# A new order for a fused attention and gated-MLP kernel: loads of q on SyncE's queue, work moved between engines

## The chip, the cores and the metric

One core of a Trainium2 chip runs the whole program. The metric is the time of one execution on the device in microseconds, the median of several runs. The engines are TensorE (PE, with its weight loads shown as PEld), VectorE (DVE), ScalarE (ACT), GpSimd (POOL) and SyncE (SP, which here only issues DMAs).

## The reference

The inputs are q, k and v of shape 4 x 8 x 768 x 64 (batch, heads, sequence, head size), a decay per head and the weights of a gated MLP. All come in float32, and so does the output of shape 4 x 768 x 512.

```python
# linear attention with decay, in blocks of 64 positions
intra = einsum('bhic,bhjc->bhij', qb, kb) * Dmask      # lam ** (i - j), causal
intra = einsum('bhij,bhjd->bhid', intra, vb)
inter = einsum('bhid,bhde->bhie', qb * lam_pow, kv_state)
out[:, :, sl] = intra + inter
kv_state = lam_block * kv_state + einsum('bhsd,bhse->bhde', kb_dec, vb)
# gated MLP with spatial mixing; x is the attention's output, 4 x 768 x 512
h = maximum(x @ w_in, 0);  u, v = halves of h
v_n = (v - mean(v)) / sqrt(var(v) + 1e-6)
v_s = einsum('ts,bsd->btd', w_spatial, v_n) + b_spatial
return (u * v_s) @ w_out
```

## The kernel before, in words

The work is cut into twelve steps of 256 positions, three for each of the four batches. Step n belongs to batch n // 3. All matmuls are in bf16.

Nothing is scheduled by a compiler: the string ORDER lists some 650 tokens, and the program issues them one after the other. A token such as `GM.0.3.0.D` is an operation (GM), its indices (batch 0, feature tile 3, half 0) and, in its last letter, the engine: T for TensorE, D for VectorE, A for ScalarE, P for GpSimd, S for a DMA that SyncE issues. Each engine works its own tokens strictly in this order; between engines, semaphores follow from which tile an instruction reads or writes. So a token that waits holds up all that stands behind it on its engine. Eight semaphores in turn tell of the landing of DMAs from SyncE and ScalarE, so one of these DMAs is issued only after the one eight before it has landed.

The operations that the text names, with their lines:

- LQ, LK, LV (`load`, L191): the float32 loads of q, k and v of one step, 512 KB each as given by the profile, into one of three buffers each.
- WI, WS, WO (L257, L262, L266): loads of the weights by GpSimd, cast to bf16. GT (`after`, L253) copies one number out of a loaded tile on GpSimd, so that the weights behind it are not asked for before that load has landed.
- WU (`w_u`, L212): filler matmuls of 256 columns on a constant tile, whose result nobody reads.
- KC, QC, QM (L178 or L176, L299): q and k to bf16 in another layout; QM also scales q. TK, TQ (L328) transpose on TensorE, EK, EQ bring the result to SBUF (EQ with the decay). From step 7 on, the DMAs DK and DQ (L305, L309) transpose instead.
- VD (L314): v scaled by the decay, in two halves; both inputs are in SBUF.
- SC (L369): the scores, two halves of a step; MK (L373): score times mask, PSUM to SBUF.
- KV (L385): the state, accumulated in PSUM bank 7; SS (L176): its copy to SBUF (`s_sb`). The next KV waits for SS, since it writes the same bank.
- AV.n.0 and AV.n.1 (L406, L415): the attention output. Between them stands SY (`apart`), a copy of two numbers on DVE or ACT, for which AV.n.1 waits. EX copies the result to SBUF as `xT`.
- PV (L438), EV, BN, RA, RD (L466 is its second instruction, with two SBUF inputs, 128x2 elements), VN: the second half of h and its normalization.
- PU (L485), EU (L443): the first half of h, transposed.
- WT, EW: the transposed spatial weights. PW (L506): the spatial matmul. GB (L511): its result plus bias, PSUM to SBUF (`vsb`, two buffers). GM (L517): `vsb` times `uT`; both inputs are in SBUF.
- PO (L522), PH (L528): the last matmul; EO, EH: its copy into one of six output tiles (`o_sb`); ST, SH: the store. An output tile is written again for the next batch, after its store.

Of the kernel before, what the change touches and what calls it, by code (L numbers as in the profile page):

```python
# [25 lines left out]
EU.0.1.3.A AV.2.0.0.T RD.0.D PU.1.0.5.T SS.2.0.A SY.2.0.D BN.1.1.D AV.2.1.0.T PU.0.0.2.T EX.2.0.0.A EX.2.1.1.D
RA.1.A VN.0.0.D VN.0.1.A PV.2.1.1.T BS.S RD.1.0.D VN.1.0.D EU.0.0.2.A PV.2.0.0.T QC.3.2.D EV.2.1.1.A VN.1.1.D
PU.2.0.6.T EV.2.0.0.A BN.2.1.D EU.1.0.5.A LK.4.2.S TQ.3.1.T BN.2.0.D EU.2.0.6.A WT.1.3.T WT.2.0.T KC.3.2.P
EQ.3.1.D RA.2.A WT.5.4.T EW.2.0.A WT.4.2.T RD.2.0.D LV.4.2.S WT.0.6.T EW.4.2.D EW.5.4.A WT.3.1.T TK.3.0.T
EW.1.3.D QC.4.2.P EW.0.6.D PU.2.1.2.T EK.3.0.A LQ.5.2.S EW.3.1.D TQ.4.6.T VN.2.1.D EU.2.1.2.A VN.2.0.D  # L30
SC.3.0.0.T VD.3.0.D SC.3.1.3.T PW.0.1.1.5.T LK.5.2.S MK.3.1.3.D PW.0.0.0.2.T GB.0.1.1.5.D LK.6.2.S GM.0.1.1.P
PW.0.0.1.4.T GB.0.0.0.2.D MK.3.0.0.D KC.4.2.P PW.0.1.0.3.T LV.5.2.S EQ.4.6.D GM.0.0.0.P PW.0.3.1.2.T
GB.0.0.1.4.D VD.3.1.P TK.4.5.T GB.0.1.0.3.D PW.0.2.0.4.T GB.0.3.1.2.D LQ.6.2.S EK.4.5.A GM.0.1.0.P KV.3.0.T
AV.3.0.0.T GM.0.0.1.P SC.4.1.2.T SS.3.0.A SC.4.0.5.T SY.3.0.D GB.0.2.0.4.D LV.6.2.S KV.3.1.T AV.3.1.0.T
QC.5.2.P MK.4.1.2.D PW.0.3.0.4.T EX.3.0.0.A EX.3.1.1.A GM.0.3.1.P MK.4.0.5.D TQ.5.0.T LQ.7.2.S KC.5.2.A
PU.3.1.1.T VD.4.1.P EQ.5.0.D SS.3.1.A TK.5.2.T VD.4.0.P GB.0.3.0.4.D PU.3.0.6.T EK.5.2.A EU.3.1.1.D KV.4.0.T
LV.7.2.S VD.5.1.P EU.3.0.6.A AV.4.0.0.T SS.4.0.D SC.5.0.4.T SY.4.0.D LK.7.2.S WO.P SC.5.1.2.T VD.5.0.P
KV.4.1.T MK.5.0.4.D AV.4.1.0.T PV.3.1.6.T LK.8.2.S EX.4.0.0.A QC.6.2.P MK.5.1.2.D EX.4.1.1.A PV.3.0.5.T
KC.6.2.A GM.0.3.0.D PV.4.1.0.T LQ.9.2.S EV.3.1.6.A TQ.6.3.T BN.3.1.D EV.4.1.0.A QM.7.1.P TK.6.1.T PU.4.1.2.T
BN.4.1.D VD.6.1.P PU.4.0.4.T EQ.6.3.D EU.4.1.2.A QM.7.0.P SS.4.1.D EV.3.0.5.A PW.0.2.1.6.T EK.6.1.D EU.4.0.4.A  # L40
VD.6.0.P KV.5.0.T GB.0.2.1.6.D AV.5.0.0.T SS.5.0.A SC.6.0.4.T GM.0.2.0.P SC.6.1.2.T SY.5.0.A KV.6.0.T
AV.5.1.0.T MK.6.1.2.D PV.4.0.6.T EX.5.1.1.A DQ.7.S EX.5.0.0.A BN.3.0.D PO.0.2.1.T KC.7.2.P MK.6.0.4.D RA.3.A
PV.5.1.0.T EV.4.0.6.A VD.7.0.P DK.7.S SS.6.0.A PV.5.0.2.T BN.4.0.D EO.0.2.1.A GM.0.2.1.P PO.0.1.4.T RD.3.D
LQ.8.2.S EV.5.0.2.A VD.7.1.P RA.4.A PO.0.0.3.T VN.3.0.D EV.5.1.0.A EO.0.1.4.A AV.6.0.5.T BN.5.0.D KV.6.1.T
ST.0.1.S PU.5.0.4.T SS.6.1.A LV.8.2.S EO.0.0.3.A SY.6.5.D RD.4.D QM.9.1.P KV.7.0.T BN.5.1.D EU.5.0.4.A
AV.6.1.5.T PO.0.5.3.T ST.0.0.S VN.4.1.D EX.6.0.5.A SS.7.0.D RA.5.A EX.6.1.6.A PU.5.1.0.T RD.5.D VN.4.0.A
SC.7.1.1.T LV.9.2.S EU.5.1.0.D VN.3.1.A SC.7.0.5.T KV.7.1.T PO.0.3.4.T MK.7.0.5.D QM.8.0.P VN.5.1.A PV.6.0.0.T
SS.7.1.D EO.0.3.4.A QM.8.1.P MK.7.1.1.D KC.8.2.A PO.0.4.5.T DQ.8.S EO.0.5.3.A PV.6.1.6.T VD.8.0.P VD.8.1.D
VN.5.0.A PU.6.1.4.T LK.9.2.S EO.0.4.5.A DK.8.S QM.9.0.P AV.7.0.1.T EV.6.1.6.A KV.8.0.T EU.6.1.4.A SY.7.1.D
BN.6.1.D AV.7.1.1.T EV.6.0.0.A PW.1.0.1.6.T DQ.9.S VD.9.1.P EX.7.1.2.A BN.6.0.D SS.8.0.A PW.1.1.0.0.T VD.9.0.P  # L50
EX.7.0.1.D LQ.10.2.S PW.1.1.1.5.T GB.1.1.0.0.D ST.0.4.S GB.1.0.1.6.D PV.7.1.3.T GB.1.1.1.5.D KC.9.2.A
GM.1.0.1.P PW.1.0.0.2.T EV.7.1.3.A GM.1.1.1.P DK.9.S RA.6.A KV.9.0.T BN.7.1.D SC.8.0.5.T GM.1.1.0.P SC.8.1.0.T
PV.7.0.3.T GB.1.0.0.2.D ST.0.2.S MK.8.1.0.D PU.7.0.4.T EV.7.0.3.A RD.6.D PU.7.1.2.T EU.7.0.4.D LK.10.2.S
BN.7.0.D PW.1.3.1.0.T ST.0.3.S QM.10.0.P RA.7.A PU.6.0.1.T VN.6.1.A RD.7.D GM.1.0.0.P GB.1.3.1.0.D
PW.1.2.1.3.T EU.6.0.1.A MK.8.0.5.D LK.11.2.S EU.7.1.2.A PW.1.2.0.4.T LQ.11.2.S SS.9.0.A GB.1.2.1.3.D ST.0.5.S
AV.8.0.0.T GM.1.2.1.P GB.1.2.0.4.D SC.9.1.2.T KV.9.1.T SY.8.0.A SC.9.0.5.T VN.7.0.A MK.9.1.2.D AV.8.1.0.T
GM.1.3.1.P PW.1.3.0.4.T EX.8.1.1.A QM.10.1.P MK.9.0.5.D EX.8.0.0.A PO.1.3.2.T VN.6.0.A DQ.10.S GB.1.3.0.4.D
PV.8.1.1.T VN.7.1.D GM.1.3.0.P GM.1.2.0.D PV.8.0.3.T LV.10.2.S EV.8.1.1.A PU.8.1.6.T EV.8.0.3.A EO.1.3.2.A
PO.1.0.4.T BN.8.0.D PO.1.1.5.T QM.11.1.P BN.8.1.D EO.1.0.4.A EU.8.1.6.A PO.1.2.0.T ST.1.0.S KC.10.2.P ST.1.3.S
RA.8.A EO.1.1.5.A RD.8.D PO.1.5.2.T ST.1.1.S VN.8.0.D VN.8.1.A PU.8.0.4.T DK.10.S EO.1.2.0.A PW.2.0.1.3.T  # L60
SS.9.1.A VD.10.0.P EU.8.0.4.A LV.11.2.S PW.2.1.1.0.T ST.1.2.S VD.10.1.P GB.2.0.1.3.D GM.2.0.1.D PO.1.4.5.T
# [523 lines left out]
```

## Time and profile before

| | us |
|---|---|
| median of 3 runs | 156.41 |
| the runs | 155.68 to 156.83 |
| the profiled execution | 155.68 |
| its span, from first to last instruction | 154.0 |
| PE busy in it | 137.1 |
| of that, 61 fillers (L212) | 9.2 |
| DVE busy | 106.1 |
| ACT busy | 89.9 |
| POOL busy | 69.8 |

The lines of the profile below start with a line of the kernel and an engine, or with a time. In a timeline, the first number is the start in us from the span's start, the second the duration. In a table of stretches, a row gives the stretch, its length, then for PE, PEld, DVE, ACT and POOL the busy time and the number of instructions, then the granted clock of TensorE, the DMA share and GB/s. The mean granted clock of TensorE was 0.989.

### The profile page before, as it was taken

Reading aid. Unit: us, or ns where it says so; the run is one execution under the profiler, and the core shown is the slowest. Engines: PE = TensorE matmul, PEld = TensorE weight load, DVE = VectorE, ACT = ScalarE, POOL = GpSimd, SP = SyncE. Lnnn points to the kernel's source line nnn. Section 1 sums busy time; section 2 is a strip of 40 time slices with the busy share of each in tenths; the row PEclk is TensorE's granted clock in tenths of the full one; section 3 lists DMA queues with packets and bytes.
Section 4 is the critical chain, followed back from the end, with each engine's and each line's share of the span. In section 5 each row is a group of like instructions: output and inputs, shape, how many; then the busy total and the mean of one; then the engine's idle time right before and its main releaser. Section 6 shows DMA issues by size and latency. Waiting matters only on the chain.

```text
span 154.0 us, 4860 instructions
## 1 busy us (share of the span) xinstructions
PE 137.1 (89%) x2060; PEld 90.5 (59%) x2075; DVE 106.1 (69%) x191; ACT 89.9 (58%) x167; POOL 69.8 (45%) x83
## 2 busy tenths in 40 slices
PE   6967774969999999839999999999999999999990
PEld 4746542456876786635565657655676756565540
DVE  1247724688999679989976778885469888748300
ACT  3968373566850677417799824678373647960270
POOL 7435650055008999827255564564644002014700
PEclk9999998799999999999999999999999999999999
DMA  3999999999999969965999997999797000052364
GB/s 91 300 290 289 237 241 235 220 281 257 281 285 285 257 169 280 235 165 105 231 282 172 245 233 184 320 201 288 164 292 172 2 6 0 0 198 79 136 231 178
DMA packets 54152, 31.25 MB, mean 203 GB/s; under 512 B 11634, under 2 KB 51058, under 8 KB 54130
## 3 DMA queue, kind: packets, MB, share of 16 engines
q1 hardware_dynamic: 49520, 27.01, 68.6%
q0 software_dynamic: 2384, 2.75, 10.3%
q10 hardware_dynamic: 2226, 1.18, 3.0%
q8 instruction: 16, 0.26, 0.7%
q14 instruction: 6, 0.05, 0.1%
HBM read 24.77 MB, written 6.29 MB: 202 GB/s over the span
## 4 chain that ended last, share of the span: by engine, by line
PE 68%; DVE 10%; DMA 9%; SPq 6%; ACT 2%; issue 2%; POOL 1%; DVEq 0%
PE ps L506 19%; PE ps L522 13%; PE ps L438 11%; PE ps L485 10%; DMA q_in<-in_q_dram 9%; SPq L191 6%; DVE gT L517 3%; PE ps L369 3%; PE ps L415 3%; DVE a_sb L373 2%; PE ps L328 2%; PE ps L385 2%; PE ps L406 2%; PE ps L498 1%; POOL vd L314 1%
## 5 line engine op out<-in xcount | busy, mean ns | idle before, releaser
L517 POOL TENSOR_TENSOR gT<-vsb,uT 128x384 bf16<-128x384 f32 x24 | 21.8, 917 | 40.1 <-DVE vsb L511 31.4
L506 PE MATMUL ps<-wt_sb,vn 128*128 128x384 bf16 x192 | 33.9, 326 | 0.0
L373 DVE TENSOR_TENSOR a_sb<-ps,m 128x1024 bf16<-128x1024 f32 x24 | 28.6, 1216 | 2.2 <-PE ps L369 1.9
L314 POOL TENSOR_TENSOR vd<-v_in,lv 128x512 bf16<-128x512 f32 x19 | 19.6, 1043 | 18.5 <-DVE a_sb L373 10.7
L506 PEld LDWEIGHTS <-vn 128*128 128x128 bf16 x192 | 18.3, 98 | 11.9
L485 PE MATMUL ps<-xT,win_sb 128*128 128x256 bf16 x192 | 24.4, 273 | 0.0
L438 PE MATMUL ps<-win_sb,xT 128*128 128x512 bf16 x87 | 23.6, 400 | 0.4
L511 DVE TENSOR_TENSOR vsb<-ps,bsp 128x384 f32<-128x384 f32 x32 | 17.2, 550 | 9.5 <-PE ps L506 9.5
L522 PE MATMUL ps<-wout_sb,gT 128*128 128x512 bf16 x86 | 21.4, 379 | 0.4 <-issue 0.2
L443 ACT ACTIVATE vh<-ps 128x512 bf16<-128x512 f32 x23 | 13.7, 596 | 13.4 <-PE ps L438 12.4
L485 PEld LDWEIGHTS <-win_sb 128*128 128x128 bf16 x192 | 18.4, 98 | 4.9
L174 ACT ACTIVATE o_sb<-ps 128x512 f32<-128x512 f32 (+1 forms) x23 | 13.1, 586 | 11.3 <-PE ps L522 11.3
L174 ACT ACTIVATE xT<-ps 128x512 bf16<-128x512 f32 x22 | 15.2, 742 | 6.6 <-PE ps L415 6.4
L453 DVE BATCH_NORM_STATS2 st<-vh 128x6 f32<-128x512 bf16 x24 | 16.3, 679 | 2.7 <-ACT vh L443 2.6
L438 PEld LDWEIGHTS <-xT 128*128 128x128 bf16 x96 | 9.2, 102 | 10.4 <-issue 1.7
L385 PE MATMUL ps<-vd,kc 64*64 64x64 bf16 x320 | 8.9, 193 | 6.2 <-DVE s_sb L176 2.9
L522 PEld LDWEIGHTS <-gT 128*128 128x128 bf16 x92 | 8.8, 98 | 9.3 <-issue 0.2
L443 ACT ACTIVATE uT<-ps 128x512 bf16<-128x512 f32 x20 | 11.7, 596 | 2.8 <-PE ps L485 2.4
L299 POOL TENSOR_TENSOR qc<-q_in,lqn 128x512 bf16<-128x512 f32 x10 | 10.7, 1071 | 5.1 <-DMA q_in<-in_q_dram 4.7
L385 PEld LDWEIGHTS <-kc 64*64 64x64 bf16 x320 | 7.4, 109 | 8.3 <-issue 7.3
L174 ACT ACTIVATE s_sb<-ps 128x256 bf16<-128x256 f32 x16 | 6.1, 382 | 8.3 <-PE ps L385 7.4
L415 PE MATMUL ps<-a_sb,vd 64*64 64x128 bf16 x384 | 10.5, 217 | 0.3 <-DVE a_sb L373 0.3
(72 smaller groups left out, 179.7 us busy)
## 6 DMA issues: line engine op xcount, KB each, us to landing
k_in<-in_k_dram SPq DMA_DIRECT2D x12, 512.0 KB, 7.1
v_in<-in_v_dram SPq DMA_DIRECT2D x12, 512.0 KB, 6.9
out_dram<-o_sb SPq DMA_DIRECT2D x23, 256.0 KB, 3.1
q_in<-in_q_dram SPq DMA_DIRECT2D x10, 512.0 KB, 7.8
wsp_raw<-in_moe_w_spatial_dram POOLq DMA_DIRECT2D x2, 576.0 KB, 11.0
q_in<-in_q_dram ACTq DMA_DIRECT2D x2, 512.0 KB, 8.1
win_sb<-in_moe_w_in_dram POOLq DMA_DIRECT2D x2, 512.0 KB, 9.7
wout_sb<-in_moe_w_out_dram POOLq DMA_DIRECT2D x1, 512.0 KB, 9.3
```

Of the source, the lines that this page charges most:

```text
L174: nc.scalar.activation(out=o, in_=i, func=AF.Copy)
L314: vec(e).tensor_tensor(out=vd[n % NCA].rearrange("p (o i w) m d -> p o i (w m) d", o=2, i=2)[o], in0=v_in[n % NIN].rearrange("p (o i w) m ...
L373: nc.vector.tensor_tensor(out=a_sb[n % NA][:, i].rearrange("p o w j x -> p (o w) (j x)"), in0=bank(b, 2).rearrange("p o (w y) -> p (o w) y ...
L385: nc.tensor.matmul(out=pkv[row(o), u], lhsT=kc[n % NCA][row(c), u, m, o, :], rhs=vd[n % NCA][row(c), 4 * o + u, m, :], start=new and u == ...
L438: nc.tensor.matmul(out=bank(b), lhsT=x[:, g % 2, c, c ^ (g // 2)], rhs=win_sb[:, g, DH:DFF], start=(g == 0), stop=(g == NCH - 1))
L443: nc.scalar.activation(out=o, in_=i, func=AF.Relu)
L453: nc.vector.bn_stats(out=st6[p2][:, t], in_=vh[p2][:, t])
L485: nc.tensor.matmul(out=pu[:, f2].rearrange("p (c x) -> p c x", c=2), lhsT=win_sb[:, g, f * P:(f + 1) * P], rhs=x[:, 4 * i + o:4 * i + 4 - ...
L506: nc.tensor.matmul(out=bank(b)[:, 0:HW], lhsT=vn[bb % 2][:, s, f * P:(f + 1) * P], rhs=wt_sb[:, s, i * HW:(i + 1) * HW], start=(s == 0), s ...
L511: nc.vector.tensor_tensor(out=vsb[(bb * 4 + f) % NVS][:, i * HW:(i + 1) * HW], in0=bank(b)[:, 0:HW], in1=bsp[:, i * HW:(i + 1) * HW], op=A ...
L517: vec(e).tensor_tensor(out=gT[bb % 2][:, f, cols], in0=vsb[(bb * 4 + f) % NVS][:, cols], in1=uT[bb % 2][:, f, cols], op=ALU.mult)
L522: nc.tensor.matmul(out=bank(b), lhsT=gT[bb % 2][:, f, t * P:(t + 1) * P], rhs=wout_sb[:, f, :], start=(f == 0), stop=(f == NCH - 1))
```

## The change

Only the string ORDER changes; every function stays. In the new order:

- LQ.0 and LQ.1 are issued by SyncE and no longer by ScalarE. SyncE's queue begins q.0, k.0, k.1, v.0, q.1, v.1, k.2, q.2, v.2 in place of k.0, k.1, v.0, v.1, k.2, q.2, v.2, beside q.0 and q.1 on ScalarE's queue.
- A second load of the weights w_in (WI.1) stands behind GT.2.1, that is behind the landing of v.1; before, that GT stood ahead of WS.0. A third GT stands ahead of WO.
- The fillers are 54 in place of 61, in other places.
- 64 tokens change their engine, among them: seven GM from DVE to GpSimd (GM.0.3.0 is one) and four from GpSimd to DVE (GM.2.1.1, GM.3.0.0, GM.3.2.0, GM.3.3.1); four VD from DVE to GpSimd, one back; five EO from ACT to DVE.
- By count, GpSimd then has 27 GM (24 before) and 22 VD (19); DVE has 5 GM (8), 2 VD (5), 6 EO (1).
- Stores that were issued early stand later among the loads, and copies into output tiles stand behind the stores that free them.
- PSUM banks (the last index of a PE token) differ in many places.

A short part of the diff; the order of each engine is what the tokens of its letter spell:

```diff
-LK.0.2.S lam.A LQ.0.2.A LQ.1.2.A pos.P LK.1.2.S LV.0.2.S idn.P WU.-8.T LB.1.T msk.P LN.1.A LL.D LX.A KC.0.2.P
-LT.0.A LV.1.2.S QC.0.2.D mkc.A WU.29.T TQ.0.6.T LK.2.2.S TK.0.1.T GT.0.1.P WI.0.P KC.1.2.D EK.0.1.A EQ.0.6.D
...
-KV.4.1.T MK.5.0.4.D AV.4.1.0.T PV.3.1.6.T LK.8.2.S EX.4.0.0.A QC.6.2.P MK.5.1.2.D EX.4.1.1.A PV.3.0.5.T
-KC.6.2.A GM.0.3.0.D PV.4.1.0.T LQ.9.2.S EV.3.1.6.A TQ.6.3.T BN.3.1.D EV.4.1.0.A QM.7.1.P TK.6.1.T PU.4.1.2.T
-BN.4.1.D VD.6.1.P PU.4.0.4.T EQ.6.3.D EU.4.1.2.A QM.7.0.P SS.4.1.D EV.3.0.5.A PW.0.2.1.6.T EK.6.1.D EU.4.0.4.A
...
+LQ.0.2.S lam.A pos.P LK.0.2.S LK.1.2.S LV.0.2.S msk.P WU.-8.T LB.3.T LN.3.A LL.D idn.P mkc.A LQ.1.2.S LX.A
+QC.0.2.D LT.0.A WU.10.T TQ.0.2.T LV.1.2.S KC.0.2.P LT.1.A EQ.0.2.D LK.2.2.S WU.10.T TK.0.0.T GT.0.1.P WI.0.P
...
+KV.4.0.T SC.5.0.2.T AV.4.0.0.T SS.4.0.A GT.2.4.P WO.P LQ.8.2.S PV.3.1.6.T SY.4.0.D MK.5.0.2.D GM.0.3.0.P
+AV.4.1.0.T EV.3.1.6.A KV.4.1.T SC.5.1.2.T EX.4.1.1.D LV.7.2.S EX.4.0.0.A PV.3.0.5.T EU.3.1.4.A SS.4.1.D
+MK.5.1.2.D VD.5.1.P KC.6.2.A TQ.6.1.T PU.4.0.4.T LQ.9.2.S VD.6.1.P EV.3.0.5.A EQ.6.1.D TK.6.2.T PV.4.1.3.T
+VD.5.0.P EK.6.2.A PU.4.1.0.T QM.7.0.P EV.4.1.3.D EU.4.0.4.A BN.3.1.D PW.0.2.1.6.T EU.4.1.0.A VD.6.0.P KV.5.0.T
...
+RA.4.A RA.3.A LV.8.2.S PO.0.2.2.T GM.0.2.1.P RD.3.D LK.8.2.S KV.6.1.T VD.7.1.P EO.0.2.2.A BN.5.0.D AV.6.0.0.T
+PU.5.0.5.T EV.5.1.4.A SY.6.0.D LK.10.2.S SS.6.1.D QM.8.1.P EO.0.0.6.D AV.6.1.0.T KV.7.0.T BN.5.1.D PO.0.5.3.T
...
+PW.1.3.0.4.T QM.10.1.P EX.8.1.1.A MK.9.1.2.D EX.8.0.0.A GM.1.2.0.P PO.1.3.5.T RA.7.A GB.1.3.0.4.D PV.8.1.2.T
+QM.10.0.P RD.7.D PV.8.0.6.T GM.1.3.0.P EV.8.1.2.A DQ.10.S PU.8.0.4.T BN.8.1.D EV.8.0.6.A ST.0.0.S VN.7.1.A
+PO.1.1.3.T BN.8.0.D LK.11.2.S VD.10.0.P EU.8.0.4.A PO.1.5.1.T VD.10.1.D RA.8.A VN.7.0.A PO.1.0.2.T RD.8.D
+EO.1.3.5.A VN.8.1.D PU.8.1.4.T VN.8.0.A ST.1.3.S EO.1.5.1.A PO.1.4.5.T EU.8.1.4.A ST.1.5.S DK.10.S
+PW.2.0.1.6.T EO.1.1.3.A EO.1.0.2.A PW.2.0.0.4.T GB.2.0.1.6.D LV.11.2.S KC.11.2.P PW.2.1.1.3.T GB.2.0.0.4.D
+GM.2.0.1.P EO.1.4.5.D DK.11.S PO.1.2.6.T GB.2.1.1.3.D GM.2.0.0.P PW.2.2.1.4.T GM.2.1.1.D EO.1.2.6.A QM.11.0.P
+AV.9.0.0.T KV.10.0.T SC.10.0.5.T SY.9.0.D GB.2.2.1.4.D SC.10.1.2.T SS.10.0.A AV.9.1.0.T MK.10.1.2.D QM.11.1.P
...
+EO.2.5.3.A GM.3.2.0.D ST.2.2.S PW.3.3.1.6.T ST.2.1.S GB.3.2.1.2.D ST.2.5.S GM.3.2.1.P PO.3.1.4.T GB.3.3.1.6.D
+PO.3.0.0.T GM.3.3.1.D EO.3.1.4.A PO.3.2.2.T EO.3.0.0.A ST.3.1.S PO.3.5.3.T EO.3.2.2.D ST.3.0.S PO.3.3.1.T
...
```

## The prediction, made before the result was known

> **What bounds the kernel now.** I read the page's busy rows first, then PE's busy time by stretch, then the waits of PE, then the chain that ended last, then DVE and POOL in order of time.
>
> ```profile
> PE 137.1 (89%) x2060; PEld 90.5 (59%) x2075; DVE 106.1 (69%) x191; ACT 89.9 (58%) x167; POOL 69.8 (45%) x83
> DMA  3999999999999969965999997999797000052364
> ```
>
> PE is busy 137.1 of 154.0 us, and 9.2 us of that are filler matmuls (line L212). The DMA row is full through the first third. So there are two regimes, a start that waits for loads and a rest in which PE sets the pace. Stretches of PE's busy time show where it stood still (times from the span's start, busy us in the second column, engine by engine):
>
> ```profile
> 20.00:32.00 12.00, 9.30 (x139) 5.51 (x141) 5.52 (x9) 6.96 (x13) 1.29 (x3) 0.86 1.16 226
> 32.50:34.10 1.60, 0.37 (x9) 0.29 (x9) 1.51 (x4) 0.60 (x1) 1.56 (x2) 1.00 0.98 278
> 59.90:64.80 4.90, 4.90 (x45) 3.45 (x43) 4.90 (x2) 3.56 (x7) 4.89 (x6) 1.00 1.19 241
> 64.80:67.80 3.00, 0.08 (x3) 0.11 (x3) 2.93 (x8) 0.00 (x0) 0.00 (x0) 1.00 0.98 268
> ```
>
> Until 34.1 us PE pauses for data. From there to its last matmul at 150.08 us it is idle for 3.8 us in all, and 2.9 of them are one hole, 64.8 to 67.8. Four views tell its cause, in this order: the waits of PE (in total us, times, longest), the chain that ended last (start, us, what), DVE in order of time, and POOL in order of time (start, us, instruction):
>
> ```profile
> PE ps L385 <- DVE s_sb L176: 2.9, 1, 2.9
> ```
>
> ```profile
> 58.92 1.22 DVE a_sb L373
> 60.14 5.07 DVE gT L517
> 65.21 0.61 DVE st L453
> ```
>
> ```profile
> 60.05 5.15 DVE L517 TENSOR_TENSOR gT<-vsb,uT 128x384 bf16<-128x384 f32 x1
> ...
> 67.31 0.41 DVE L176 CAST s_sb<-ps 128x256 bf16<-128x256 f32 x1
> ```
>
> ```profile
> 59.89 1.04 POOL L299 TENSOR_TENSOR qc<-q_in,lqn 128x512 bf16<-128x512 f32 x1
> 60.89 1.03 POOL L314 TENSOR_TENSOR vd<-v_in,lv 128x512 bf16<-128x512 f32 x1
> 61.89 1.03 POOL L299 TENSOR_TENSOR qc<-q_in,lqn 128x512 bf16<-128x512 f32 x1
> 62.89 1.03 POOL L314 TENSOR_TENSOR vd<-v_in,lv 128x512 bf16<-128x512 f32 x1
> 63.89 0.90 POOL L517 TENSOR_TENSOR gT<-vsb,uT 128x384 bf16<-128x384 f32 x1
> ```
>
> The multiply GM.0.3.0 stands on DVE. It takes 5.15 us where the median of its kind on DVE is 0.58, and it ends just after POOL's unbroken row of five instructions ends at 64.79. So a DVE instruction that takes both inputs from SBUF waits until POOL pauses. Behind it on DVE stands the state copy SS.4.1 (67.31), for which PE's KV.5.0 waits. The 1216 ns evictions from PSUM (L373) show no such stretching.
>
> The start ends with the third load of v:
>
> ```profile
> 32.02 2.04 POOL L314 TENSOR_TENSOR vd<-v_in,lv 128x512 bf16<-128x512 f32 x2 [10.73 <-DVE a_sb L373]
> 33.10 0.31 PE L385 MATMUL ps<-vd,kc 64*64 64x64 bf16 x8 [0.55 <-POOL vd L314]
> 34.11 0.25 PE L385 MATMUL ps<-vd,kc 64*64 64x64 bf16 x5 [0.69 <-POOL vd L314]
> ```
>
> That load is asked for at 12.35 and takes 19.5 us to land, so it lands at 31.87; POOL starts 0.15 later (the named releaser, a DVE eviction, ends at the same moment). Two vd multiplies of 1.02 us follow, then KV.2.0.
>
> **The change part by part.** The arithmetic stays; what moves is order and engine. I work on the profiled execution, 155.68 us (span 154.0, 1.7 around it). The runs' median is 156.41, 0.73 more; I add that at the end.
>
> *The hole at 65 us.* GM.0.3.0 goes to POOL, and SS.4.1 now stands on DVE right behind MK.5.0, EX.4.1, ahead of MK.5.1 and the BN pair. No DVE instruction with two SBUF inputs is left in that stretch, so POOL's row can be as long as it likes. POOL carries 0.91 us more there; VD.5.0, which KV.5.0 also needs, then ends some 3 us ahead of PE by POOL's rows (1.04 a multiply, 0.91 a GM). The hole goes: -2.9, bounds -2.9 to -2.0 should VD.5.0 be a little late.
>
> *The start.* q of steps 0 and 1 moves from ScalarE's queue to SP's. On SP it stands ahead of, and between, the first k and v, and k, v of these steps move back by one or two loads; ScalarE loses two issues of 0.5 us. A load of 512 KB takes 1.78 us when one queue runs alone (landings at 12.48, 14.26 and 16.02), and 12:14 shows 290 GB/s on SP's queue. So q.0 lands near 5.4 (was 7.5) and the first PE work comes 1 to 2 us earlier. That is worth nothing by itself: work ahead of KV.2.0 is 12.3 us of PE's in both orders, and KV.2.0 still waits for v.2, the ninth 512 KB load in both. The cover is the wait for v.2; without it, the gain of 1 to 2 us would show. What can move v.2 are POOL's weight loads. Behind the landing of k.1 the first is asked for about 1.1 us earlier; the second is now gated by v.1 and comes about 0.8 later. While they run, both queues together move 226 GB/s (20:32), of which SP gets a part, so their shift can push v.2 either way: I take 0, bounds -1.5 to +1.0. Fillers fall from 61 to 54; at 0.15 us each that is under cover of the same wait.
>
> *POOL is fuller.* VD on POOL goes from 19 to 22 (3 x 1.04) and GM from 24 to 27 (3 x 0.92): +5.9 us with nothing taken away, over 154 us with 84 idle. DVE loses GM (8 to 5) and VD (5 to 2) and gains five output copies (0.69 each). The totals bind nowhere; what counts is where a DVE instruction with two SBUF inputs meets a row of POOL's. There are two such places.
>
> First, RD.3 and its small two-input instruction (L466):
>
> ```profile
> 33.02 1.06 DVE L466 SCALAR_TENSOR_TENSOR nmr<-mv,rstd 128x2 f32<-128x2 f32 x1
> ```
>
> 0.16 us of work took 1.06 beside POOL's vd pair. In the new order RD.3 meets QM.7.1, VD.7, GM.0.2.1, QM.8, QM.9.1 on POOL, and behind it on DVE stand BN.5.0 and SY.6.0, for which AV.6.1 on PE waits. By the rows RD.3 comes about 1 us before POOL pauses and AV.6.1 about 1.5 us after: +0.2, bounds 0 to +1.5.
>
> Second, GM.2.1.1, now on DVE in step 10. Count from the start of PW.2.0.1 (108.4 before). PE reaches AV.9.1 after four PW of 0.975, one PO of 0.865, AV.9.0, KV.10.0 and SC.10, at 5.8 us. DVE has evicted PW.2.1.1 at 3.65. POOL runs GM.2.0.1 (1.7), GM.2.0.0, QM.11.0, QM.11.1 without a gap and pauses at 5.65. GM.2.1.1 then ends at 6.2, SY.9.0 at 6.35, and AV.9.1 is late by 0.6. If DVE gets in ahead of QM.11.0 it is 0; if KC.11 on POOL is late as well, it is 2: +0.6, bounds 0 to +2.
>
> The Trainium skill, "SBUF — State Buffer", section "Who interferes with whom", has the pair of ports that DVE and GpSimd share held "for the whole instruction" by whoever comes first. By that rule a DVE instruction would wait for one POOL instruction, 1.04 us at most, GM.2.1.1 would end at 5.2 and the sum would be 0.6 less. The row above has one waiting through five.
>
> *DK.10 behind stores.* On SP the transposing load DK.10 now stands behind ST.1.3 and ST.1.5, whose copies on ScalarE stand behind VN.7.1, RA.8, VN.7.0 and VN.8.0. I make its issue -0.1 on the same count. The like one before went out at 107.6 and landed 4.9 us later, so it lands at 4.85, and SC.10.0 needs it at 5.3: 0, bounds 0 to +1.
>
> *The tail.* Work behind the last PW is the same five PO and two halves. ST.3.1's copy now waits until ST.2.1 is out (six output tiles, so EO.3.t waits for ST.2.t), which bunches the last stores: PE's end at 150.08 to the span's end was 3.9 us; I add 0.2, bounds 0 to +0.8.
>
> Sum: -2.9 + 0 + 0.2 + 0.6 + 0 + 0.2 = -1.9. 155.68 - 1.9 = 153.8 for an execution like the profiled one, 154.5 for the median. With likely bounds of the terms this forecast's own range is 152.5 to 155.6.
>
> **The rivals.** *The gain is given back in small waits.* A new order of 650 steps has other tight pairs than the two above; at each AV.n.0 to AV.n.1 pair DVE's SY copy must come within about 0.9 us. For: DVE is busy 17.5 of the 20 us from 44 to 64. Against: after 68 us PE is idle only 0.8 us in the old order. With 1.5 us of them on top: 156.0.
>
> *Slower: POOL's row before GM.2.1.1.* k.11 is moved behind DQ.10 and ST.0.0 on SP. DQ.10 waits for QM.10.0, which now waits for GM.1.2.0. On PE's time less the hole, QM.10.0 ends at 97.7, LK.11 goes out at 99.5 and, with the 5.8 us it took before, lands at 105.3, against PW.2.0.1 at 105.5. Each us that it lands later than that shifts KC.11, GM.2.0.1, GM.2.0.0, QM.11.0 and QM.11.1 as one unbroken row of 5.0 us, then GM.2.1.1, SY.9.0 and AV.9.1. The loss equals k.11's lateness behind PW.2.0.1: from 2.5 us on the whole gain is gone, and at 4.5 the time is 158.4. For: before, some loads took 15 to 19 us to land. Against: these did so beside weight loads, and none are left then.
>
> *Faster: v.2 lands earlier.* If the later gate of the second weight load leaves SP's queue alone for longer, KV.2.0 starts 1.5 us or more sooner: 153.0 or less. For: SP alone moves 290 GB/s. Against: what it gains is owed to the weights soon after.
>
> That the change doesn't do what it says can be excluded for GM.0.3.0, which stands on POOL.
>
> **How the numbers follow.** Forecast 0.45, small waits 0.25, slower 0.15, v.2 earlier 0.15. 1% (1.56 us) is about what a measurement of this kernel can tell from no change, so faster is below 154.85 and slower above 157.97. Faster: 0.36 of the forecast and all of v.2 earlier, 0.51. Same: 0.09 of the forecast and 0.22 of the small waits, 0.31. Slower: 0.15 and 0.03 of the small waits, 0.18. The range, 152.3 to 158.0, leaves out about 1 in 10 on either side.
>
> **What would show it.** Right: no DVE line of L517 near 5 us, no PE wait for s_sb of 2.9 us; KV.2.0's second half still near 34.1; a hole of about half a us in front of AV.9.1; PE's end near 148.2. Wrong: KV.2.0 moved by over 1.5 us, another hole of over 1 us behind 68 us, above all before AV.6.1, SC.10.0 or AV.9.1.

## The result, and the profile after

The changed kernel takes 148.17 us, the median of four runs (147.31 to 149.19); the kernel before, in four runs, 156.62 (155.68 to 157.28). The ratio is 0.947, with a 95% interval of 0.939 to 0.955. The prediction was 154.5, with a range of 152.3 to 158.0, so the change brought some four times what was forecast. The ratios here leave out runs that lie more than 1.5% above the fastest of their kernel; where the times of a kernel fall into two groups, all of them are given.

The profiled execution took 147.31 us, its span 145.6. First the busy row, the granted clock and the DMA row of its page:

```profile
PE 134.3 (92%) x2051; PEld 88.6 (61%) x2068; DVE 98.4 (68%) x191; ACT 87.6 (60%) x160; POOL 75.9 (52%) x90
...
PEclk9999999999999999999999999999999999999999
DMA  3999999999999999999999999789992120050574
```

TensorE (PE) keeps its full clock throughout, and the DMA row is full for its first two thirds; before, it has dips behind the first third. The same stretches as before, in the same columns:

```profile
20.00:32.00 12.00, 11.31 (x201) 7.57 (x203) 9.32 (x21) 10.00 (x20) 4.26 (x5) 1.00 1.17 230
59.90:64.80 4.90, 4.85 (x127) 2.99 (x123) 4.69 (x8) 3.10 (x7) 4.14 (x6) 1.00 1.27 292
64.80:67.80 3.00, 3.00 (x46) 1.63 (x45) 2.02 (x8) 1.98 (x6) 3.00 (x4) 1.00 0.91 173
```

The hole at 64.8 is gone. The surprise is the first row: from 20 to 32 us PE works 11.31 us, before 9.30. POOL and PE in order of time (start, duration) say why:

```profile
25.65 2.04 POOL L314 TENSOR_TENSOR vd<-v_in,lv 128x512 bf16<-128x512 f32 x2 [3.43 <-DMA v_in<-in_v_dram]
```

```profile
27.29 0.60 PE L485 MATMUL ps<-xT,win_sb 128*128 128x256 bf16 x4
27.82 0.38 PE L385 MATMUL ps<-vd,kc 64*64 64x64 bf16 x12
```

v.2 lands at 25.48 us, before at 31.87. KV.2.0 starts at 27.82 straight behind other work of PE; before, its second half started at 34.11 after two waits. That gives the account of the two profiled executions:

| stretch | before | after | difference |
|---|---|---|---|
| start to KV.2.0 (before: its second half) | 34.11 | 27.82 | -6.29 |
| KV.2.0 to PE's end (150.04, 141.69) | 115.93 | 113.87 | -2.06 |
| PE's end to the span's end (153.97, 145.61) | 3.93 | 3.92 | 0 |

The second row is the hole of 2.9 less new small waits: outside the hole PE stood still for 0.9 us there before and for 1.8 after. The first row, three quarters of the gain, stood in the prediction as 0.

Where do 6.4 us of v.2's landing come from? Tables of stretches of two us (the last number is GB/s) show the weight loads as bursts. Before:

```profile
16.00:18.00 2.00, 1.71 (x73) 1.27 (x72) 1.23 (x3) 0.16 (x1) 1.24 (x2) 1.00 1.19 209
18.00:20.00 2.00, 0.92 (x51) 0.69 (x42) 2.00 (x2) 1.41 (x4) 1.39 (x2) 1.00 1.16 313
20.00:22.00 2.00, 1.95 (x67) 1.25 (x67) 0.14 (x1) 1.24 (x4) 1.29 (x3) 1.00 1.20 218
22.00:24.00 2.00, 0.75 (x24) 0.49 (x12) 0.00 (x0) 2.00 (x4) 0.00 (x0) 1.00 1.17 233
24.00:26.00 2.00, 0.76 (x9) 0.76 (x10) 0.69 (x1) 0.47 (x1) 0.00 (x0) 0.88 1.17 236
```

After:

```profile
14.00:16.00 2.00, 1.52 (x44) 1.17 (x45) 1.11 (x2) 0.92 (x2) 1.66 (x3) 1.00 1.21 219
16.00:18.00 2.00, 1.24 (x87) 1.08 (x75) 1.67 (x2) 1.21 (x3) 1.30 (x2) 1.00 1.13 307
18.00:20.00 2.00, 1.65 (x44) 1.03 (x45) 1.17 (x3) 1.70 (x4) 0.48 (x1) 1.00 1.17 293
20.00:22.00 2.00, 2.00 (x38) 1.13 (x36) 0.72 (x2) 2.00 (x5) 2.00 (x3) 1.00 1.21 237
22.00:24.00 2.00, 1.74 (x28) 1.08 (x29) 1.97 (x5) 1.20 (x3) 0.22 (x1) 1.00 1.20 224
24.00:26.00 2.00, 1.65 (x36) 0.97 (x37) 1.97 (x4) 1.97 (x4) 0.35 (x1) 1.00 1.18 275
```

Stretches near 215 GB/s are bursts of POOL's weights (WI.0, then WI.1, then WS.1 and WS.0), stretches near 300 are gaps in which SP's loads of q, k and v run almost alone. The view of the DMA queues gives the shares, first for 16 to 18, then for 18 to 20 us, before (q0 is POOL's queue, q1 that of SP; packets, MB, share of the 16 engines):

```profile
q0 software_dynamic: 291, 0.30, 89.1%
q1 hardware_dynamic: 236, 0.12, 29.7%
...
q1 hardware_dynamic: 1110, 0.56, 96.3%
q0 software_dynamic: 79, 0.07, 19.6%
```

In the first of these stretches, a burst, SP moves 0.12 MB in two us, in the second, mostly a gap, 0.56: one us of gap is worth nearly five of a burst. Between the bursts of WI.0 and WI.1 the gap lasts from about 18.4 to 20.0 us before, from 16.5 to 20.3 after. WI.0 is asked for at 9.07, before at 10.78, since it waits for k.1, which lands at 8.90, before at 10.08; WI.1 is asked for at the same time (15.44, before 15.39). And WS.1 is asked for at 20.50, before 19.59, which leaves a second gap near 24 us.

One more thing lies in the packets. Each DMA engine ends its part of a transfer with a packet of 4 bytes, and in each weight load one of the 16 comes after the rest, before by 0.5 to 1.3 us (in the last load two are late): for WI.0, fifteen from 18.0 to 18.8 us and one at 20.0. If that is an engine that is late, it sees no gap at all, since WI.1 starts at 20. On SP's queue fifteen such packets follow from 19.2 to 19.8 (q.2), then none until 23.4. The semaphores of the two loads count their sixteen parts: of q.2, fifteen have landed by 20.3 us and the last at 24.40; of v.2, fourteen by 24.6, one at 25.98, and the last, which is v.2's landing, at 31.87. After the change the last part of q.2 lands at 21.19 and that of v.2 at 25.48. I read this as one late engine; the trace does not name engines.

### The profile page after: what moved, and what is told of

Read it like the earlier page. It is cut to its first block, busy times and chain, and to the rows that moved or that the text cites. A ratio compares the mean times of both kernels' runs of the same rounds, so it can differ in the third digit from the quotient of the medians.

```text
span 145.6 us, 4855 instructions
## 1 busy us (share of the span) xinstructions
PE 134.3 (92%) x2051; PEld 88.6 (61%) x2068; DVE 98.4 (68%) x191; ACT 87.6 (60%) x160; POOL 75.9 (52%) x90
## 3 DMA queue, kind: packets, MB, share of 16 engines
HBM read 24.77 MB, written 6.29 MB: 213 GB/s over the span
## 4 chain that ended last, share of the span: by engine, by line
PE 78%; DMA 9%; SPq 6%; DVE 3%; issue 1%; ACT 0%; DVEq 0%
PE ps L506 22%; PE ps L485 15%; PE ps L522 12%; PE ps L438 12%; DMA q_in<-in_q_dram 7%; SPq L191 6%; PE ps L369 4%; PE ps L415 3%; PE ps L385 3%; PE ps L328 3%; PE ps L406 2%; PE ps L498 1%; DMA out_dram<-o_sb 1%; DVE o_sb L176 1%; DVE qc L176 0%
## 5 line engine op out<-in xcount | busy, mean ns | idle before, releaser
L517 POOL TENSOR_TENSOR gT<-vsb,uT 128x384 bf16<-128x384 f32 x27 | 24.6, 920 | 26.8 <-DVE vsb L511 26.7
L314 POOL TENSOR_TENSOR vd<-v_in,lv 128x512 bf16<-128x512 f32 x22 | 23.1, 1061 | 15.6 <-DMA v_in<-in_v_dram 10.7
L438 PE MATMUL ps<-win_sb,xT 128*128 128x512 bf16 x84 | 21.8, 379 | 0.9 <-issue 0.5
L443 ACT ACTIVATE vh<-ps 128x512 bf16<-128x512 f32 x21 | 12.5, 598 | 12.2 <-PE ps L438 11.3
L174 ACT ACTIVATE o_sb<-ps 128x512 f32<-128x512 f32 (+1 forms) x18 | 10.2, 586 | 15.7 <-PE ps L522 13.0
L174 ACT ACTIVATE xT<-ps 128x512 bf16<-128x512 f32 x21 | 14.7, 744 | 3.7 <-PE ps L415 3.5
L443 ACT ACTIVATE uT<-ps 128x512 bf16<-128x512 f32 x23 | 13.5, 594 | 3.7 <-PE ps L485 3.7
L178 POOL CAST kc<-k_in 128x1024 bf16<-128x1024 f32 x7 | 7.3, 1037 | 10.8 <-DMA k_in<-in_k_dram 5.7
L212 PE MATMUL ps<-warm 128*128 128x256 bf16 x54 | 8.7, 319 | 1.7 <-DVE warm L210 1.3
L369 PE MATMUL ps<-qT,kT 64*64 64x128 bf16 x384 | 9.1, 218 | 0.4 <-issue 0.3
```

The source lines that it names most:

```text
L174: nc.scalar.activation(out=o, in_=i, func=AF.Copy)
L314: vec(e).tensor_tensor(out=vd[n % NCA].rearrange("p (o i w) m d -> p o i (w m) d", o=2, i=2)[o], in0=v_in[n % NIN].rearrange("p (o i w) m ...
L369: nc.tensor.matmul(out=pa[row(c), o, w, j], lhsT=kT[n % NTR][row(o), u, j, c * Q64:(c + 1) * Q64], rhs=qv(n, o, u, c), start=True, stop=True)
L438: nc.tensor.matmul(out=bank(b), lhsT=x[:, g % 2, c, c ^ (g // 2)], rhs=win_sb[:, g, DH:DFF], start=(g == 0), stop=(g == NCH - 1))
L443: nc.scalar.activation(out=o, in_=i, func=AF.Relu)
L517: vec(e).tensor_tensor(out=gT[bb % 2][:, f, cols], in0=vsb[(bb * 4 + f) % NVS][:, cols], in1=uT[bb % 2][:, f, cols], op=ALU.mult)
```

## The experiments

The diffs show only the tokens around an edit. The time behind "against" is the median of seven runs of the kernel before, taken beside that group of experiments.

The theory: v.2 lands when the slowest engine has moved q.2 and v.2, and it does so mostly in the gaps between the bursts of weights; the change widened a gap by letting WI.0 go earlier, and the rest of the 650 steps did not matter for it. The first rival: one queue for q, k and v is what helps, in itself. The second: the weights' later gate (GT.2.1 ahead of WI.1). The third, from the prediction: the hole is the gain.

**e1: GM.0.3.0 alone.** In the order before:

```diff
-KC.6.2.A GM.0.3.0.D PV.4.1.0.T
+KC.6.2.A GM.0.3.0.P PV.4.1.0.T
```

> The order before with one letter changed: GM.0.3.0 on GpSimd. By the prediction's own term the hole at 65 us goes and nothing else moves: PE has no wait for s_sb of 2.9 us, the time falls by 2.9 us (155.7 to 152.8 for executions alike, ratio 0.981), v.2 still lands near 31.9. Rival: the hole is only one of several delays behind one another and the saving is used up by GpSimd's row, which is one multiply longer: -1 us or less. If this alone gave -8 the start would have nothing to do with the change's gain.

152.07 us (151.72 to 154.05) against 156.69: -4.6 by medians. The wait for `s_sb` of 2.9 us is gone; in its profile KV.2.0 to PE's end takes 113.38 us in place of 115.93, so the hole is worth 2.5 us, and v.2 landed at 30.76, 1.1 us earlier than in the profile of before; in e8 the unchanged order shows a scatter of that size. The prediction's term holds for this edit. By medians the edit gives about half of the gain, by the term itself 2.5 us.

**e2: q on SP alone.**

```diff
-LK.0.2.S lam.A LQ.0.2.A LQ.1.2.A pos.P LK.1.2.S LV.0.2.S idn.P
+LQ.0.2.S LK.0.2.S lam.A pos.P LK.1.2.S LV.0.2.S LQ.1.2.S idn.P
```

> The order before with the loads of q of steps 0 and 1 on SyncE at the new order's places, and nothing else. The prediction's term was 0 (v.2 lands near 31.9). Theory A (one queue in the order of need is what brings v.2 forward, by itself or through the weights being asked for later): v.2 lands at 25 to 27 and the time falls by 5 to 6.5 us, ratio 0.96. Theory B (the second gate, GT.2.1 ahead of WI.1, or the other moved weights are what brings it forward): v.2 lands at 30 to 32 and the time falls by under 1.5 us.

148.40 us (147.58 to 149.85) against 156.69. v.2 landed at 25.46. Two moved loads give the whole gain; the gate GT.2.1 (theory B) is not needed for it. And the hole is gone too, with GM.0.3.0 still on DVE: it takes 0.55 us here.

**e3: both.**

```diff
-LK.0.2.S lam.A LQ.0.2.A LQ.1.2.A pos.P LK.1.2.S LV.0.2.S idn.P
+LQ.0.2.S LK.0.2.S lam.A pos.P LK.1.2.S LV.0.2.S LQ.1.2.S idn.P
...
-GM.0.3.0.D
+GM.0.3.0.P
```

> Both edits on the order before: q of steps 0 and 1 on SyncE, GM.0.3.0 on GpSimd. If the two places explain all of the change's gain, this order is within 1 us of the changed kernel, 147.3 to 149 us, ratio 0.945 to 0.955. If the other some 60 moved tokens carry part of it, it stays above 150.

149.46 us (147.10 to 150.63) against 156.69: no better than e2. The two gains do not add up: KV.2.0 to PE's end takes 112.63 us here and 113.42 in e2, so of GM.0.3.0's 2.5 us 0.8 is left, and the rest is contained in the earlier start. The profile (149.58) shows why the time is no lower: v.2 landed at 25.53, but the granted clock was 0.50 from 20.4 to 27.2 us, and KV.2.0 started at 31.32 behind the work that this made late. Here the first gap is about as short as before (18.8 to 19.8 us), and the one before the spatial weights is longer (23.3 to 25.1).

**e4 and e10: the changed order with q back on ScalarE.**

```diff
-LQ.0.2.S lam.A pos.P
+lam.A LQ.0.2.A LQ.1.2.A pos.P
...
-LQ.1.2.S
```

> The changed order with the loads of q of steps 0 and 1 put back on ScalarE, at the places that they had. Theory A: v.2 lands at 30 to 32 again, and the time is 153 to 155 us, ratio 0.98 to 0.99. Theory B: v.2 stays at 25 to 27 and the time at 148 to 149 us, ratio 0.95.

Two times near 149 (149.02, 149.77) and two near 155.5 (155.41, 155.52), against 156.69. The profiled one, 155.52, has v.2 at 30.97. WI.0 was asked for at 10.10 us, between the two orders. It was run once more for a second profile:

> The changed order with q on ScalarE once more, for a second profile: it gave two times near 149 and two near 155.5, WI.0 being asked for at 10.1 us, between the 10.6 to 10.8 of the order before and the 9.1 of the change. If 10.1 lies on the edge, a time near 149 goes with v.2 at 25 to 27 and a time near 155.5 with v.2 at 30 to 32. If the time comes out near 149 with v.2 at 31, the two times have another cause.

149.18 us, with v.2 at 28.27, so the fast group does not need v.2 at 25. The landing differs by 2.7 us, the time by 6.3. PE at KV.2.0 (start, duration, idle before), then stretches, first of e4:

```profile
33.23 0.53 PE L385 MATMUL ps<-vd,kc 64*64 64x64 bf16 x12 [4.08 <-POOL vd L314]
```

```profile
30.00:32.00 2.00, 0.00 (x0) 0.00 (x0) 0.00 (x0) 0.00 (x0) 0.86 (x1) 0.99 1.13 247
32.00:34.00 2.00, 0.77 (x34) 0.76 (x37) 0.00 (x0) 0.04 (x1) 1.68 (x3) 0.50 1.12 313
34.00:36.00 2.00, 2.00 (x26) 1.31 (x18) 0.93 (x3) 1.34 (x3) 1.26 (x2) 0.50 1.15 233
36.00:38.00 2.00, 2.00 (x31) 1.33 (x30) 0.85 (x3) 0.81 (x2) 1.35 (x2) 0.50 0.88 257
```

and of e10:

```profile
30.53 0.38 PE L385 MATMUL ps<-vd,kc 64*64 64x64 bf16 x13 [0.87 <-POOL vd L314]
```

In e4 PE stands still for 4.08 us; the granted clock falls to 0.50 at about 32 us and stays there until 38.8. In e10 it waits 0.87 us and the clock stays at 1.00 there. KV.2.0 to PE's end is 116.66 us in e4 and 113.03 in e10, 3.6 us more. Of these, 2.5 fall between KV.2.0 and the first PW (33.23 to 46.26 in e4, 30.53 to 41.08 in e10), where the slow matmuls are. Another 1.05 us falls at the place that the prediction had named, RD.3 with its small instruction, first in e4, then in e10:

```profile
73.19 2.30 DVE L466 SCALAR_TENSOR_TENSOR nmr<-mv,rstd 128x2 f32<-128x2 f32 x1
```

```profile
68.00 0.27 DVE L466 SCALAR_TENSOR_TENSOR nmr<-mv,rstd 128x2 f32<-128x2 f32 x1
```

In e4 it ends as POOL's row of three multiplies does (72.44 to 75.48), and AV.6.1 behind it comes about 1 us later. In e7 and e13, where v.2 is late too, it takes 2.31 and 2.29 us.

**e5: WI.0 earlier, nothing else.** In the order before, q on ScalarE, GM.0.3.0 on DVE:

```diff
-GT.0.1.P WI.0.P
+GT.1.0.P WI.0.P
```

> The order before, with q still on ScalarE; only the first weight load (WI.0) is let go by the landing of q.0 (GT.1.0, 7.5 us) in place of that of k.1 (10.1), so that it is asked for near 7.7 us, before at 10.8 and with the change at 9.1. Theory A1 (what helps is that the first weights come earlier: their burst on the 16 DMA engines ends earlier, and a gap opens ahead of the burst of WI.1 in which k, q and v run at full rate): v.2 lands at 25 to 27 and the time falls by 4 to 7 us, ratio 0.96 to 0.975. Theory A2 (one queue for k, q and v matters in itself): v.2 lands at 30 to 32, ratio 0.99 to 1.01.

147.97 us (147.56 to 149.21) against 157.10, ratio 0.949 (0.939 to 0.960). v.2 landed at 25.55. One token gives what the whole new order gives. Its stretches in the gap:

```profile
16.00:18.00 2.00, 1.71 (x66) 1.25 (x68) 1.23 (x3) 0.22 (x2) 1.12 (x2) 1.00 1.14 292
18.00:20.00 2.00, 1.05 (x60) 0.83 (x49) 2.00 (x2) 1.27 (x4) 0.38 (x1) 1.00 1.17 298
```

WI.0 was asked for at 8.22 us; the gap opens near 16.9 us, about as it does after the change. One queue for q, k and v is not needed (theory A2 falls).

**e6: the spatial weights later.** In the order before:

```diff
-WS.1.P
+GT.1.2.P WS.1.P
```

> The order before, with a wait for the landing of q.2 (GT.1.2) put ahead of WS.1, so that the spatial weights are asked for near 24.5 us in place of 19.6. Their burst then starts near 29 and not near 24.5, and v.2 has the gap for itself. If v.2 is held up by the spatial weights, as A1 and its twin (only their later request counts) have it: v.2 lands at 26 to 27, the transposes of the spatial weights near 40 us wait little, and the time falls by 4 to 6 us, ratio 0.965. A2: v.2 at 30 to 32, ratio 0.99 to 1.01.

148.50 us (148.05 to 149.46) against 157.10, ratio 0.952 (0.943 to 0.962). WS.1 was asked for at 24.13, v.2 landed at 25.73. Here the gap before WI.1 is as short as before (WI.0 at 10.57), but the next one lasts until 27:

```profile
24.00:26.00 2.00, 1.79 (x15) 1.09 (x16) 1.28 (x3) 0.77 (x2) 1.96 (x5) 1.00 1.16 320
26.00:28.00 2.00, 1.85 (x39) 1.01 (x39) 1.93 (x5) 1.71 (x3) 1.92 (x2) 1.00 1.19 267
```

A gap elsewhere does as well.

**e7: the spatial weights earlier, in the changed order** (GpSimd's tokens alone).

```diff
-KC.2.2.P WS.1.P WS.0.P
+WS.1.P WS.0.P KC.2.2.P
```

> The changed order with WS.1 and WS.0 ahead of KC.2.2 on GpSimd, asked for near 17.4 us in place of 20.5, so that their burst joins that of WI.1. A1 (gaps between bursts): q.2 still in time near 21, v.2 no longer finds the gap at 24 and lands at 27 to 31; the time rises by 2 to 6 us against the changed kernel, ratio to the order before 0.96 to 0.985. A2: v.2 stays at 25.5 and the ratio at 0.945.

152.11 us, the median of six times from 149.64 to 154.92, against 157.10. In the profile, 154.92, v.2 landed at 30.56, PE waited 4.79 us for it, and the clock was at 0.50 from 31.2 to 38.0 us. WI.0 was early (8.82), q on SP and the first gap as long as in the changed kernel (17.7 to 20.1 free of weights): without the second gap that is not enough.

**e8: the order before, unchanged.**

> The order before, unchanged, profiled once more. If the stall of GM.0.3.0 behind GpSimd's row is fixed by the order, a multiply of about 5 us and a hole of 2.9 us are there again; if it hangs on a fraction of a microsecond, GM.0.3.0 takes under 2 us this time. v.2 lands within 1 us of 31.9 if the start is as steady as the loads alone on the queue are; if it lands near 25, the late landing itself comes and goes from run to run.

155.48 us, v.2 at 30.20. The stall of GM.0.3.0 is there again, DVE first and then POOL:

```profile
59.74 5.28 DVE L517 TENSOR_TENSOR gT<-vsb,uT 128x384 bf16<-128x384 f32 x1
```

```profile
59.69 1.04 POOL L299 TENSOR_TENSOR qc<-q_in,lqn 128x512 bf16<-128x512 f32 x1
60.70 1.04 POOL L314 TENSOR_TENSOR vd<-v_in,lv 128x512 bf16<-128x512 f32 x1
...
63.70 0.90 POOL L517 TENSOR_TENSOR gT<-vsb,uT 128x384 bf16<-128x384 f32 x1
```

So in the order before, with its late start, the unbroken row on POOL and the hole come back. v.2 landed 1.7 us earlier than in the first profile of this order, and yet the time is the same, since here the granted clock fell behind the wait:

```profile
32.00:34.00 2.00, 1.56 (x35) 1.26 (x35) 0.45 (x2) 0.38 (x1) 0.38 (x1) 0.59 1.08 316
34.00:36.00 2.00, 2.00 (x32) 1.27 (x30) 0.48 (x2) 0.00 (x0) 0.62 (x1) 0.56 0.99 250
```

KV.2.0 to PE's end took 117.42 us in place of 115.93. Against this profile the changed kernel's gain is 4.6 us at the start and 3.6 behind it.

**e9: WI.1 later.** In the order before (GpSimd's tokens alone):

```diff
-VD.1.0.P WI.1.P VD.1.1.P
+VD.1.0.P VD.1.1.P WI.1.P
```

> The order before with WI.1 behind VD.1.1 on GpSimd, asked for near 17.3 us in place of 15.4; WI.0, the spatial weights and the queues of q as before. In every trace so far one of the 16 DMA engines is some 1.2 us behind the other 15 in each weight transfer, and 15 parts of v.2 are there near 24 while the sixteenth decides. Theory L (what matters is that this late engine too sees a gap between the bursts of WI.0 and WI.1, wherever it lies): the gap grows from 1.6 to 3.5 us, the late engine gets through q.2 and most of v.2 in it, v.2 lands at 24 to 27, ratio 0.945 to 0.965, although the bursts of WI.1 and WS.1 now touch. Theory M (the first weights must be earlier or the spatial weights later): v.2 at 30 to 32, ratio 0.99 to 1.01.

Four times, 148.72, 149.36, 154.94 and 158.08, against 156.43; the profile is of the second, with v.2 at 28.79. WI.1 moved by only 1.0 us (16.38), not by 1.9 as I had reckoned, and the result lies between the theories: inconclusive.

**e11: GM.0.3.0 on DVE in the changed order.**

```diff
-GM.0.3.0.P
+GM.0.3.0.D
```

> The changed order with GM.0.3.0 back on DVE, in the same place, where EX.4.1 and SS.4.1 stand behind it. If a multiply there waits for the whole of GpSimd's row, it takes 3 us or more and the hole of 2 to 3 us is back: 150 to 151 us, ratio to the order before 0.96 to 0.965. If it waits for one instruction at most, it takes under 1.6 us and the time stays within 0.6 us of the changed kernel's, ratio 0.945.

147.59 us (147.19 to 149.30) against 156.43, ratio 0.946 (0.935 to 0.957): the same as the changed kernel. DVE, then POOL:

```profile
53.76 0.54 DVE L517 TENSOR_TENSOR gT<-vsb,uT 128x384 bf16<-128x384 f32 x1
```

```profile
52.04 0.79 POOL L266 DMA_DIRECT2D wout_sb<-in_moe_w_out_dram  x1
55.07 3.04 POOL L314 TENSOR_TENSOR vd<-v_in,lv 128x512 bf16<-128x512 f32 x3 [2.24 <-DMA v_in<-in_v_dram]
```

The multiply meets a pause of POOL's, which waits there for v. With an earlier start POOL has caught up with its loads, the long row is broken, and the move of GM.0.3.0 is worth nothing.

**e12: WI.0 earlier still, in the changed order.**

```diff
-GT.0.1.P WI.0.P
+GT.1.0.P WI.0.P
```

> The changed order with WI.0 let go by q.0 (5.3 us) in place of k.1, so asked for near 8.2 us, when KC.0 on GpSimd is done, in place of 9.1. If the gap in front of WI.1 is already long enough in the changed order, v.2 lands at 25 to 26 as there and the time stays within 0.7 us of it, ratio 0.943 to 0.949; if the start still waits for weights, the first PV on TensorE comes 0.8 us sooner and the time falls by as much, ratio 0.94.

148.06 us (147.24 to 149.05) against 156.43, ratio 0.946 (0.937 to 0.956), v.2 at 25.47. WI.0 was asked for at 8.12. No gain: the gap was long enough.

**e13: WI.0 late, in the changed order.**

```diff
-GT.0.1.P WI.0.P
+GT.2.0.P WI.0.P
```

> The changed order with WI.0 let go by v.0 (10.7 us) in place of k.1 (8.9), so asked for near 10.8 us, as in the order before; q stays on SyncE, everything else as changed. If the time of the first weight request carries the whole gain at the start (A1), the gap in front of WI.1 closes, v.2 lands at 28 to 32 and the time rises to 149 to 155 us, ratio 0.95 to 0.99. If q on SyncE's queue has a share of its own, v.2 stays near 25.5; only the first PV, which needs WI.0, then comes up to 2 us later, 148 to 150 us.

154.86 us (153.84 to 155.22) against 156.34. v.2 landed at 31.77:

```profile
31.94 2.04 POOL L314 TENSOR_TENSOR vd<-v_in,lv 128x512 bf16<-128x512 f32 x2 [12.12 <-DMA v_in<-in_v_dram]
```

WI.0 was asked for at 11.36; k.2 then landed as its burst began (16.18, in the changed kernel 19.40), so WS.1 went out earlier too (18.24), and both gaps closed. One token takes back the gain of nearly all the others, with q on SP and GM.0.3.0 on GpSimd. The first PV waits 2.3 us for WI.0, but PE then still waits 3.1 us for v.2 before KV.2.0, so that wait is covered.

**e14: WI.1 much later.** In the order before (GpSimd's tokens alone):

```diff
-VD.1.0.P WI.1.P VD.1.1.P KC.2.2.P WS.1.P
+VD.1.0.P VD.1.1.P KC.2.2.P WI.1.P WS.1.P
```

> The order before with WI.1 behind KC.2.2 on GpSimd, asked for near 19.6 us in place of 15.4, the spatial weights right behind it. The burst of WI.0 ends at 18.4 (15 engines) and 20.0 (the late one), the next begins near 24. Theory L (a gap that the late engine sees too is enough, wherever it lies): v.2 lands at 22 to 25, earlier than in any run so far, without WI.0 being earlier, and the bursts behind it touch; the time is 147.5 to 151 us, ratio 0.945 to 0.97, more if PU.1.1 waits for WI.1, which lands near 29. Theory M (the first weights must be earlier or the spatial weights later): v.2 at 28 or more, 152 us or more.

148.70 us (148.19 to 149.10) against 156.34. Stretches, then POOL:

```profile
18.00:20.00 2.00, 1.14 (x67) 0.92 (x57) 1.98 (x2) 1.19 (x3) 1.16 (x2) 1.00 1.15 315
20.00:22.00 2.00, 1.77 (x52) 1.02 (x55) 1.05 (x2) 1.25 (x4) 2.00 (x3) 1.00 1.16 293
22.00:24.00 2.00, 2.00 (x44) 1.55 (x45) 0.55 (x2) 1.99 (x4) 1.62 (x3) 1.00 1.21 250
```

```profile
23.15 2.04 POOL L314 TENSOR_TENSOR vd<-v_in,lv 128x512 bf16<-128x512 f32 x2 [0.38 <-DMA v_in<-in_v_dram]
```

WI.0 is late (10.45) and the spatial weights go out about when they did (20.61), but the gap in front of WI.1 now lasts from 18.4 to 22.8 us, and v.2 lands at 23.01, the earliest of all. Theory L stands, M falls: the gap is the cause, not the order of the weights in time. v.2 at 23 gains nothing over 25.5, since PE has other work until 27.8 or later; here KV.2.0 starts at 29.93, after a wait of 1.1 us for WI.1.

| kernel | WI.0, WI.1, WS.1 asked for | v.2 lands | KV.2.0 | KV.2.0 to PE's end | median us |
|---|---|---|---|---|---|
| before | 10.78, 15.39, 19.59 | 31.87 | 34.11 | 115.93 | 156.62 |
| changed | 9.07, 15.44, 20.50 | 25.48 | 27.82 | 113.87 | 148.17 |
| e2 q on SP | 9.28, 15.11, 20.41 | 25.46 | 28.98 | 113.42 | 148.40 |
| e5 WI.0 early | 8.22, 15.27, 20.60 | 25.55 | 28.84 | 114.75 | 147.97 |
| e6 WS late | 10.57, 15.31, 24.13 | 25.73 | 29.77 | 113.36 | 148.50 |
| e14 WI.1 late | 10.45, 19.82, 20.61 | 23.01 | 29.93 | 113.57 | 148.70 |
| e7 WS early | 8.82, 15.20, 17.01 | 30.56 | 32.82 | 116.48 | 152.11 |
| e13 WI.0 late | 11.36, 15.44, 18.24 | 31.77 | 34.03 | 114.18 | 154.86 |

No version beats the changed kernel by more than can be measured: e5, e11 and e12 lie within 0.6 us of it. With v.2 in time and the clock at full speed, PE sets the pace from about 19 us on, and the rest of the new order finds nothing to gain there. The spread of the order before is large, in one set of seven from 149.38 to 159.87. Its two profiles, with v.2 at 31.87 and 30.20, and the two of e4 and e10 suggest the same cause, a load that makes or misses a gap and a clock that falls behind the wait; this is not shown, since neither end of that range was profiled.

## Why the prediction was wrong, step by step

**The start, the step that failed.** "What can move v.2 are POOL's weight loads ... I take 0, bounds -1.5 to +1.0." The cause was named and the sign left open; the size was wrong: -6.29, four times the lower bound. Three parts of the working went wrong.
- The bound has the size of the shift of the requests, about 1 us either way (the first 1.1 earlier, the second 0.8 later; measured 1.7 earlier and 0.05 later). A shift of the first request by 1.7 us went with one of v.2 by 6.4, because time in a gap is worth nearly five times as much as time in a burst (0.56 MB against 0.12 in two us), and because the last of 16 parts sets the landing. The figure of 226 GB/s for both queues together hid this: the rows of 16 to 18 and 18 to 20 us, one by one, had it.
- "Against: what it gains is owed to the weights soon after." It is owed only if v.2 is not through by then. In the changed order v.2 is through as the burst of the spatial weights begins.
- The rival "v.2 lands earlier" had the right place at 0.15, but named the later gate of the second weight load, which did nothing (15.39 and 15.44), and not the earlier first one.

The cover that the prediction named, the wait for v.2, is what went, and it said that the gain of 1 to 2 us in the first loads "would show" without it.

**The hole, -2.9 with bounds to -2.0.** Right in size: -2.5 in e1. Wrong in what removes it once the start moves: in e2 and e11 the multiply on DVE takes 0.55 and 0.54 us; in e11 it meets a break in POOL's row.

**POOL fuller.** RD.3's small instruction took 0.68 us beside POOL, and PE lost 0.3 us in all between 66 and 80: the +0.2 holds. With a late v.2 it is 2.3 us, and AV.6.1 is about 1 us late (e4, e7, e13), inside the bound of 1.5. GM.2.1.1, priced at +0.6, cost nothing:

```profile
103.78 1.31 DVE L517 TENSOR_TENSOR gT<-vsb,uT 128x384 bf16<-128x384 f32 x1
```

```profile
103.63 2.36 POOL L299 TENSOR_TENSOR qc<-q_in,lqn 128x512 bf16<-128x512 f32 x2
```

It waited for one POOL instruction (QM.11.0), then went ahead of the second, which was stretched to 1.4 us; SY.9.0 came at 105.20 and PE had no hole. The rule of the Trainium skill ("SBUF — State Buffer", "Who interferes with whom") that I set against the row was right here. In the row of five it fails twice, 5.15 and 5.28 us, and RD.3 with its 2.3 us in e4 waits through two starts of POOL's instructions as well. What tells the two cases apart stays open.

**DK.10 and the tail.** DK.10 cost 0, as said: PE works 9.95 of the 10 us from 98 to 108. The tail is 3.92 us, before 3.93, not +0.2.

**The other rivals.** Small waits ate 0.9 us of the gain, where the rival had 1.5: from KV.2.0 to its end PE works 112.03 of 113.87 us, before 112.10 of 115.93 with the hole of 2.9. k.11's lateness played no part: no hole stands before AV.9.1.

Sum of the steps behind KV.2.0: -2.1 forecast (without the tail), -2.06 measured, with one term too dear by 0.6 and small losses in its place, so that the agreement to the tenth is luck. Nearly the whole miss is the start.

## What to carry to other kernels

When casting weight loads and operand loads share the DMA engines, look at the traffic in steps of one or two us and find the gaps between the bursts: a load that just misses a gap waits for the whole next burst, so its landing moves by several times the shift of a request. Price such a step by both cases, through in this gap or in the next, not by an average rate. And before paying for a new order of everything, try the gates of the few large loads: here one token did as much as 650.

## What was not expected of the hardware

- Sharing between queues. In a burst SP's queue got 0.12 of 0.42 MB, although it had loads waiting. The Trainium skill, "DMA: Bandwidth & Descriptors", section "SWDGE vs HWDGE vs iDMA", has each DMA engine go round its queues in turn; the packets of the profile are 512 bytes on SP's queue and 1024 on POOL's in that stretch, and 236 packets of SP against 291 of POOL's would fit such a turn.
- One of the 16 DMA engines, in some loads two, was late in the weight loads of every trace, if the late part is an engine's: the last part landed 0.35 to 1.84 us after the median one. The same page, section "Latency and other measured facts", calls two of the 16 usually slower. The trace does not show which one it is. A transfer of 16 KB of instructions, 0.9 to 1.2 us long, falls into the first bursts too. In four traces (before, e1, e8, e10) one weight load has no such transfer beside it, and there the last part lands 0.35 to 0.57 us after the median one, in their other weight loads 0.8 to 1.7. That points to it as part of the cause; it was not tried.
- A PE wait of 4.08 us was followed by a granted clock of 0.50 for 6.8 us, most of them after the wait, and the stretch to the first PW took 2.5 us longer (e4 against e10). A wait of 3.14 us in e13 was not: the clock stayed at 1.00. The Trainium skill, "TensorE: Matmul & The Clock Gate", section "What's actually happening", has the clock halved after an idle window of about 3.4 us; the waits of 4.08 and 4.79 us here agree. But the clock also fell where no wait was so long: in e8 at 32.3 us, behind 3.4 us in which PE worked 1.55 and waited at most 1.26 at a time, and in e3 at 20.4, behind 3.4 us with 1.85 of work. What share of work keeps the clock up is not shown.
